# Linear attention and a gated MLP on one core: one query layout for all batches, k^T v copied once, listed buffers and another written order

## The chip, the core and the metric

The kernel runs on one core of a Trainium2 chip. Five engines work on their own instruction queues: TensorE (PE, matrix products, with its weight loads listed as PEld), VectorE (DVE), ScalarE (ACT), GpSimd (POOL) and SyncE (SP), which here only issues DMAs. The time is that of the device, in microseconds (us), from one launch; lower is better.

## The reference, cut to what matters

Eight batches (b), eight heads, 576 tokens, head dimension 64. The first half is a linear attention without softmax, the second an MLP with a gate over the tokens:

```
kv  = einsum('bhsd,bhse->bhde', k, v)          # 64 x 64 per head
out = einsum('bhsd,bhde->bhse', q, kv)
x   = out / sqrt(mean(out*out, -1) + 1e-6) * g_norm     # then (b, 576, 512)
h   = gelu_tanh(x @ w_in);  u, v = h[..., :512], h[..., 512:]
v_n = (v - mean) / sqrt(var + 1e-6) * g_ln
v_s = einsum('ts,bsd->btd', w_sg, v_n) + b_sg
y   = x + (u * v_s) @ w_out
```

## The kernel before

Everything is written out by hand. A string `ORDER` lists some 1,890 steps; a step is a letter, the batch, a number and sometimes the engine (v for DVE, a for ACT, p for POOL), and each becomes one or a few instructions at the end of its engines' queues. No scheduler moves them. An engine takes its instructions in that order and waits where an operand or a buffer is not ready.

The steps that this text speaks of, batch by batch:

- `k` and `q` load keys, values and queries; `D` loads a piece of the weights. All are issued by SP in the written order.
- `K` makes k^T v: 64 x 64 products of PE, two at a time in the two column halves, summed over the tokens in one PSUM bank (`pkv`). `c` (`kv_copy`) copies that to SBUF (`kvf`). Before, four copies per batch of 64 x 256 put each head's block where `o` wants it.
- `o` multiplies kvf with the queries (PSUM tiles `pq` in batch 0, `po` in the others); `e` squares the result on ACT, `f` scales it into `x`, `s` sums the squares over each head by products with ones (`psq`, `pss`), `t` makes the reciprocal root in small DVE steps.
- In batch 0 the roots are spread over the partitions by a product (`M`, tile `pb`) and `x` multiplies. In the other batches `r0` writes the rows to DRAM (`rd`), and further `r` read them back broadcast: `bc` for two tiles of x, and `bc` again, in the same buffer, for the other two; `bl` for the last 64 tokens.
- `X` and `Y` split x into a high part (`xh`) and the rest (`xo`), since the products run in the one-pass form of fp32 (fp32r) as three products each.
- `U` and `V` (12 matmuls each, `pu` 128x288 and `pv` 128x512) are x @ w_in; `S` (14 matmuls, `pg`) the product over the tokens; `P` (`py`, 12 matmuls) the output product with seven blocks instead of eight. `g`, `G`, `H`, `J`, `R`, `h`, `W` make the gated operand between S and P; `Q` and `Z` add py to x; `O` stores.
- `A` `B` `E` `L` `C` `F` `I` turn the words of the weights into their high and low parts on ACT, DVE and POOL, piece by piece. U needs pieces 0 to 3 of w_in, V pieces 4 to 7.
- `N` is a product of zeros into a bank that nobody reads (`warm`): it only keeps PE busy. There are 78.

Batches overlap: while batch b is in S and P, batch b+1 is in U and V, and K, o, s of b+2 lie between. PSUM has four banks `ps`, two `po`, two `pa`; a tile takes the next bank of its tag in turn. The 28 buffers `h` of 128x288 are listed by number in `HOMES`.

In batch 0 the queries come in another layout than in the others (two lines of the launch code), since there one tile of q holds one half of the tokens for two pairs of heads, so that half of the work can begin after two of the four loads.

## Time and profile before

| | |
|---|---|
| median of 3 runs | 500.01 us (499.13 to 500.21) |
| the profiled execution: its time | 499.58 us |
| its span (first to last instruction) | 497.8 us |
| PE busy | 487.7 us, 98% |
| DVE, ACT, POOL busy | 72%, 36%, 33% |

Times of rows count from the first instruction of the span. "Busy" of PE is taken from starts and modelled ends of matmuls, so it holds pipeline latency too. An fp32 product is listed as two rows (two passes), an fp32r product as one. In a row of the timeline, the bracket at the end gives the idle time of the engine before the row and who ended it.

### The profile page before, as it was taken

How to read it: one execution, taken by the hardware profiler on the slowest of the kernel's cores; microseconds unless marked ns; L12 is line 12 of the kernel's file. 1: busy time of each engine (PE TensorE's matmuls, PEld its weight loads, DVE VectorE, ACT ScalarE, POOL GpSimd, SP SyncE). 2: the span in 40 equal slices, each digit the busy share in tenths (PEclk: the TensorE clock that was granted, in tenths of full speed). 3: DMA queues.
4: the chain of work that ended last, by engine and by line, in shares of the span. 5: the costliest groups of instructions: out<-in, count | busy, mean ns of one | idle time of the engine just before them, and what ended most of it. 6: DMA issues, size and time to landing. Idle time of an engine off the chain costs nothing.

```text
span 497.8 us, 10129 instructions
## 1 busy us (share of the span) xinstructions
PE 487.7 (98%) x3998; PEld 442.6 (89%) x3998; DVE 357.6 (72%) x830; ACT 181.4 (36%) x443; POOL 164.7 (33%) x206
## 2 busy tenths in 40 slices
PE   6999999999999999999999999999999999999997
PEld 6568888999988999889998898998998799989996
DVE  2388799888886776578565788557757777557576
ACT  1478677245235312242233215124223523122121
POOL 2232235541354222522253133362153205432350
PEclk9999999999999999999999999999999999999999
DMA  8996786220543563002736325100240033000014
GB/s 232 362 324 222 208 251 183 75 90 20 176 116 114 141 181 112 1 1 78 203 118 201 101 80 180 35 1 25 60 163 0 2 84 91 0 2 0 1 49 166
DMA packets 33658, 55.36 MB, mean 111 GB/s; under 512 B 7308, under 2 KB 9228, under 8 KB 33612
## 3 DMA queue, kind: packets, MB, share of 16 engines
q1 hardware_dynamic: 33612, 54.73, 36.1%
q8 instruction: 31, 0.51, 0.4%
q14 instruction: 15, 0.12, 0.1%
HBM read 44.76 MB, written 9.95 MB: 110 GB/s over the span
## 4 chain that ended last, share of the span: by engine, by line
PE 87%; DVE 6%; DMA 3%; ACT 2%; issue 1%; SPq 0%
PE pg L639 20%; PE pu L625 19%; PE pv L574 18%; PE py L700 17%; PE pkv L365 4%; PE pg L642 3%; PE po L398 3%; PE pss L443 2%; DMA v<-in_vl 1%; DMA kv_first<-in_vx 1%; DVE g L668 1%; DMA q<-in_qT 1%; DVE xo L543 1%; PE warm L221 1%; PE psq L427 1%; PE pb L511 1%
## 5 line engine op out<-in xcount | busy, mean ns | idle before, releaser
L652 POOL TENSOR_TENSOR u<-gt,u 128x288 f32<-128x288 f32 x64 | 56.6, 893 | 98.7 <-DVE gt L647 96.2
L639 PE MATMUL pg<-wsh,vh 128*128 128x288 f32 x256 | 76.0, 297 | 0.0
L639 PE MATMUL pg<-wso,vh 128*128 128x288 f32 x256 | 75.6, 295 | 0.0
L639 PE MATMUL pg<-wsh,vo 128*128 128x288 f32 x256 | 75.5, 295 | 0.0
L713 DVE SCALAR_TENSOR_TENSOR x<-py,x 128x288 f32<-128x288 f32 x112 | 48.7, 452 | 20.3 <-PE py L700 19.7
L668 DVE TENSOR_TENSOR g<-u,g 128x288 fp32r<-128x288 f32 x112 | 53.8, 499 | 10.3 <-ACT g L176 8.1
L647 DVE SCALAR_TENSOR_TENSOR gt<-pg,glt,b_bc 128x288 f32<-128x288 f32 x64 | 32.3, 513 | 35.3 <-PE pg L642 35.2
L630 ACT ACTIVATE u<-pu 128x288 f32<-128x288 f32 x64 | 25.8, 410 | 85.3 <-PE pu L625 84.5
L700 PE MATMUL py<-g,woh 128*128 128x288 f32 x256 | 55.9, 296 | 1.0 <-DVE x L713 1.0
L176 ACT CAST g<-u 128x288 fp32r<-128x288 f32 x72 | 29.7, 433 | 62.5 <-POOL u L652 30.3
L639 PEld LDWEIGHTS pg<-wsh,vh 128*128 128x128 f32 x256 | 48.1, 188 | 0.9 <-DVE gt L647 0.4
L639 PEld LDWEIGHTS pg<-wso,vh 128*128 128x128 f32 x256 | 48.1, 188 | 0.1
L639 PEld LDWEIGHTS pg<-wsh,vo 128*128 128x128 f32 x256 | 48.2, 188 | 0.0
L625 PE MATMUL pu<-xh,wuh 128*128 128x288 f32 x256 | 45.4, 299 | 0.0
L625 PE MATMUL pu<-xo,wuh 128*128 128x288 f32 x256 | 44.5, 295 | 0.0
L625 PE MATMUL pu<-xh,wuo 128*128 128x288 f32 x256 | 44.3, 295 | 0.0
L700 PEld LDWEIGHTS py<-g,woh 128*128 128x128 f32 x256 | 42.8, 188 | 1.7 <-DVE x L713 1.4
L589 POOL TENSOR_SCALAR rs<-mv 128x1 f32<-128x1 f32 x36 | 12.7, 353 | 88.4 <-DVE mv L585 87.7
L700 PE MATMUL py<-g,wxh 128*128 128x288 f32 x192 | 41.4, 298 | 0.4 <-DVE g L668 0.4
L625 PEld LDWEIGHTS pu<-xh,wuh 128*128 128x128 f32 x256 | 37.9, 188 | 3.2 <-issue 1.0
L579 ACT ACTIVATE hv<-pv 128x512 f32<-128x512 f32 x32 | 19.0, 597 | 55.1 <-PE pv L574 51.9
L700 PE MATMUL py<-g,woo 128*128 128x288 f32 x128 | 37.8, 295 | 0.0
(124 smaller groups left out, 1043.8 us busy)
## 6 DMA issues: line engine op xcount, KB each, us to landing
q<-in_qT SPq DMA_DIRECT2D x32, 288.0 KB, 5.3
out_y<-x SPq DMA_DIRECT2D x28, 288.0 KB, 2.3
bc<-rd SPq DMA_DIRECT2D x28, 256.0 KB, 4.4
k<-in_kx SPq DMA_DIRECT2D x24, 256.0 KB, 4.0
v<-in_vx SPq DMA_DIRECT2D x24, 256.0 KB, 4.4
words<-in_wu SPq DMA_DIRECT2D x4, 512.0 KB, 3.8
kv_first<-in_kx SPq DMA_DIRECT2D x8, 256.0 KB, 6.4
kv_first<-in_vx SPq DMA_DIRECT2D x8, 256.0 KB
```

The costliest lines, as they stand in the source:

```text
L176: e.copy(dst, src) if e is ac else e.tensor_copy(dst, src)
L365: nc.tensor.matmul(part["kv", b][64 * r : 64 * r + 64, p * 64 : p * 64 + 64], k_[b, c][:, h], v_[b, c][:, h], start=(c == 0 and p == 0), s ...
L574: nc.tensor.matmul(pv, a[cc], w[:, cc, :], start=(n == 0), stop=(n == 11))
L579: ac.activation(hv_[b, c], pv_[b, c], AF.Gelu_apprx_tanh, scale=W_UP)
L625: nc.tensor.matmul(pu[:, :HS], w[:, cc, f], a[b, cc][:, t], start=(i == 0), stop=(i == 11))
L630: ac.activation(u_[b, n], part["u", b, n][:, :HS], AF.Gelu_apprx_tanh, scale=W_UP)
L639: nc.tensor.matmul(ps[:, :HS], a[:, d], w[:, c, t], start=(i == 0), stop=False)
L647: ve.scalar_tensor_tensor(g_[b, n], ps[:, :HS], glt[:, dc : dc + 1], b_bc[:, half(n // 4)], op0=ALU.mult, op1=ALU.add)
L652: po.tensor_tensor(u_[b, n], g_[b, n], u_[b, n], op=ALU.mult)
L668: ve.tensor_tensor(lo, src, f32(hi), op=ALU.subtract)
L700: nc.tensor.matmul(y_[b, bank][c][:, :HS], wo_block(h, blk, e)[:, block(c)], a, start=(start and i == 0), stop=(i == 5), skip_group_check= ...
L713: ve.scalar_tensor_tensor(xs, y_[b, bank][c][:, :HS], W_UP, xs, op0=ALU.mult, op1=ALU.add)
```

## The change

The query layout of batch 0 is taken for all batches: tile 2r + p//2 of q holds the half r of the tokens for the pairs p of heads. In `K` the head of a product is chosen so that heads land in the partition half in which `o` reads them. So k^T v leaves PSUM in one copy of 128 x 256 per batch (8 copies, not 32), kvf is half as large, and one step `o(b, n)` of a batch b > 0 makes one half of the tokens for all four pairs, from two tiles of q, where before it made both halves of two pairs. The number of products is the same. Successive products of `o` now go to the array's quarters (rows 0-63, columns 0-63), (0-63, 64-127), (64-127, 0-63), (64-127, 64-127); before, to (0-63, 0-63), (64-127, 0-63), (0-63, 64-127), (64-127, 64-127). Batch 0 had the new sequence already.

All tags with several buffers, the PSUM banks among them, now have a list in `HOMES` that says which buffer each tile takes. The buffers of tag `x` are 12, not 11. `ORDER` is written anew from end to end, with 51 steps `N`, not 78.

```diff
@@ T, PS
+    turn = {tag: iter(homes.split()) for tag, homes in HOMES.items()}
     def T(shape, dtype, tag, bufs=1, nm=None):
-        return sb.tile(shape, dtype, tag=tag, bufs=bufs, name=nm or tag)
+        home = tag + next(turn[tag]) if bufs > 1 else tag
+        return sb.tile(shape, dtype, tag=home, bufs=1, name=nm or tag)
     def PS(nm, tag="ps"):
-        return pp.tile([P, 512], F32, tag=tag, bufs=BANKS[tag], name=nm)
+        return pp.tile([P, 512], F32, tag=tag + next(turn[tag]), bufs=1, name=nm)
@@ kv
-            for p in range(NP):
+            for n in range(NP):
                 for r in range(2):
-                    h = slice(p * P + 64 * r, p * P + 64 * r + 64)
+                    h = slice((n // 2 * 2 + r) * P + n % 2 * 64, (n // 2 * 2 + r) * P + n % 2 * 64 + 64)
@@ kv_copy
-        if not n:
-            part["kvf", b] = T([P, NP, P], F32, "kvf", 2)
-        src = part["kv", b][64 * h : 64 * h + 64, : NP * 64].rearrange("a (p e) -> a p e", p=NP)
-        cast(e, part["kvf", b][64 * r : 64 * r + 64, :, 64 * h : 64 * h + 64], src)
+        part["kvf", b] = T([P, NP * 64], F32, "kvf", 2)
+        cast(e, part["kvf", b], part["kv", b][:, : NP * 64])
@@ o
-        for p in (n % 4,) if b == 0 else (2 * n, 2 * n + 1):
+        r = n // 4 if b == 0 else n
+        for p in (n % 4,) if b == 0 else range(NP):
...
+                    part["kvf", b][d, (p // 2 * 2 + h) * 64 : (p // 2 * 2 + h) * 64 + 64],
+                    q_[b, 2 * r + p // 2][d, half(h)],
@@ launch
-    qT = q.reshape(B, NP, 2, 2, HS, D).transpose(0, 1, 3, 5, 2, 4).copy()
-    qT[0] = qT[0].transpose(1, 0, 2, 3, 4).reshape(qT[0].shape).copy()
+    qT = q.reshape(B, NP, 2, 2, HS, D).transpose(0, 3, 1, 5, 2, 4)
@@ ORDER, its first line
-    D00 q00 k04 D21 D23 k00 k01 N899 N898 N897 ...
+    D00 A00 k04 B00a E00 L00 C00 k01 F00a D21 I00v F21 D23 k03 k00 N899 N898 N897 ...
```

Three places show how instructions move. The first is the head of SP's queue, the order in which the first loads are issued (`words` are weight pieces, `kv_first` keys and values of batches 0 and 1, `k<-in_kl` their last 64 tokens). Before:

```order
L238 DMA words<-in_wu 128x2x512
L385 DMA q<-in_qT 128x576
L356 DMA k<-in_kl 64x512
L356 DMA v<-in_vl 64x512
L246 DMA gnt<-in_gn 128x1
L251 DMA glt<-in_gl 128x4
L356 DMA kv_first<-in_kx 128x512
L356 DMA kv_first<-in_vx 128x512
```

and now:

```order
L289 DMA words<-in_wu 128x2x512
L407 DMA k<-in_kl 64x512
L407 DMA v<-in_vl 64x512
L407 DMA kv_first<-in_kx 128x512
L407 DMA kv_first<-in_vx 128x512
L297 DMA gnt<-in_gn 128x1
L302 DMA glt<-in_gl 128x4
L407 DMA kv_first<-in_kx 128x512
```

The first tile of q moved from second place to behind the last keys and values of batch 0 and one more piece of words.

The second is the head of PE's queue, up to the first products of U (`pb` spreads the roots of batch 0, `pkv` is batch 1's k^T v, `po` batch 1's output, `pss` its sums of squares). Before:

```order
L365 MATMUL pkv<-kv_first 64x64 x16
L365 MATMUL pkv<-v,k 64x64 x8
L511 MATMUL pb<-rstd,ext 128x288
L398 MATMUL po<-q,kvf 64x288 x8
L443 MATMUL pss<-sq,ones 32x144 x4
L398 MATMUL po<-q,kvf 64x288 x8
L625 MATMUL pu<-xh,wuh 128x288 x4
```

and now:

```order
L416 MATMUL pkv<-kv_first 64x64 x8
L416 MATMUL pkv<-v,k 64x64 x8
L554 MATMUL pb<-rstd,ext 128x288
L441 MATMUL po<-q,kvf 64x288 x8
L668 MATMUL pu<-xh,wuh 128x288 x4
L668 MATMUL pu<-xh,wuo 128x288 x4
L668 MATMUL pu<-xo,wuh 128x288 x4
L668 MATMUL pu<-xh,wuh 128x288 x4
L668 MATMUL pu<-xh,wuo 128x288 x4
L668 MATMUL pu<-xo,wuh 128x288 x4
L441 MATMUL po<-q,kvf 64x288 x8
```

The second half of batch 1's `po` and the first four products of its `pss` moved behind the first two U.

The third is DVE's queue between the roots of batch 0 and the last `xo` ahead of the first U (`x<-x,pb` scales batch 0's x, `x<-po` scales batch 1's, `w_...` and `wuo` are weight pieces). Before:

```order
L524 TENSOR_TENSOR x<-x,pb 128x288 x4
L543 TENSOR_TENSOR xo<-x,xh 128x288
L524 TENSOR_TENSOR x<-x,pb 128x288
L277 TENSOR_SCALAR w_356<-w_356 128x512
L524 TENSOR_TENSOR x<-x,pb 128x288
L281 SCALAR_TENSOR_TENSOR w_356<-words,w_356 128x512
L176 COPY kvf<-pkv 64x4x64 x2
L524 TENSOR_TENSOR x<-x,pb 128x288 x2
L420 TENSOR_SCALAR x<-po,g_66 128x288 x3
L543 TENSOR_TENSOR xo<-x,xh 128x288 x2
L334 TENSOR_TENSOR wuo<-w_333,wuh 128x2x256
L543 TENSOR_TENSOR xo<-x,xh 128x288 x2
```

and now:

```order
L567 TENSOR_TENSOR x<-x,pb 128x288 x7
L232 CAST xh<-x 128x288
L328 TENSOR_SCALAR w_326<-w_326 128x512
L586 TENSOR_TENSOR xo<-x,xh 128x288
L232 CAST xh<-x 128x288
L385 TENSOR_TENSOR wuo<-w_278,wuh 128x2x256
L586 TENSOR_TENSOR xo<-x,xh 128x288 x4
```

The two copies of kvf, three scalings of batch 1 and one step on a weight piece left this stretch; two casts came in from ACT.

Further back, the written order decides how much PE work lies between a batch's last `s` and its first U or V, that is, what PE has to do while the roots go through DRAM (counted in the order list):

| batch | before | now |
|---|---|---|
| 1 | 6 U, 5 V and three K steps | 5 U, 5 V and three K steps |
| 2 | 8 S, 3 P, K40, o30 | 8 S, 2 P, K40, o30 |
| 4 | 8 S, 6 U, 6 P, 1 V, o50, K60 | 8 S, 2 P, K61, o50 |

## Rows read from the trace of the kernel before

**Rows 1.** Busy time of PE, PEld, DVE, ACT and POOL (instructions in brackets) in three stretches, then granted clock, DMA share and GB/s: batch 0 up to its roots, from there to the first U, and the rest of the span. The first column is the stretch, the second its length.

```profile
16.80:27.30 10.50, 10.11 (x61) 4.43 (x60) 6.89 (x16) 7.99 (x19) 2.71 (x2) 1.00 1.06 355
27.30:40.04 12.74, 12.57 (x141) 7.80 (x142) 10.91 (x26) 10.08 (x23) 4.31 (x4) 1.00 1.05 326
40.04:497.80 457.76, 452.23 (x3659) 418.60 (x3656) 337.21 (x778) 161.15 (x400) 154.91 (x194) 1.00 0.31 94
```

**Rows 2.** PE's timeline behind the first U: the four places where a stream of fp32r products stood still, with the idle time and who ended it.

```profile
149.46 0.74 PE L574 MATMUL pv<-wvh,xo 128*128 128x512 f32 x2 [0.42 <-DVE xo L543]
...
179.36 0.40 PE L700 MATMUL py<-g,woh 128*128 128x288 f32 x1 [0.46 <-DVE x L713]
...
291.86 0.40 PE L700 MATMUL py<-g,woh 128*128 128x288 f32 x1 [0.51 <-DVE x L713]
...
488.08 0.53 PE L700 MATMUL py<-g,wxh 128*128 128x288 f32 x2 [0.39 <-DVE g L668]
```

**Rows 3.** PE's timeline from K of batch 0 to the first U: start, us, line, output and operands, rows of the trace in it.

```profile
14.37 1.22 PE L221 MATMUL warm<-zeros 128*128 128x256 f32 x8
...
16.12 0.68 PE L365 MATMUL pkv<-v,k 64*64 64x64 f32 x16
...
17.52 0.83 PE L398 MATMUL pq<-q,kvf 64*64 64x288 f32 x4
...
22.57 0.71 PE L398 MATMUL pq<-q,kvf 64*64 64x288 f32 x8
...
38.06 0.74 PE L443 MATMUL pss<-sq,ones 128*32 128x144 f32 x8 [0.17 <-ACT sq L410]
38.73 1.38 PE L398 MATMUL po<-q,kvf 64*64 64x288 f32 x16
40.04 0.79 PE L625 MATMUL pu<-xh,wuh 128*128 128x288 f32 x4
```

**Rows 4.** SP's timeline, its issues (start, us of the issue): the last main load of batch 0, the second and third q, and the last main load of batch 1.

```profile
8.37 0.87 SPq L356 DMA_DIRECT2D kv_first<-in_vx  x1
...
9.76 1.19 SPq L385 DMA_DIRECT2D q<-in_qT  x2
...
22.51 0.33 SPq L356 DMA_DIRECT2D kv_first<-in_vx  x1
```

**Rows 5.** The loads of keys and values in the first 30 us (all of line L356): us from the start of an issue to its landing.

```profile
DMA to landing us min/median/max: 4.4/5.6/8.2
```

**Rows 6.** DVE's timeline in the head: the last step of batch 0's roots, a step on a weight piece, the first four scalings of x, and the last two `xo` of the tiles that the first U reads.

```profile
29.14 0.45 DVE L467 SCALAR_TENSOR_TENSOR rstd<-rstd 32x288 f32<-32x288 f32 x1
29.62 0.69 DVE L281 SCALAR_TENSOR_TENSOR w<-words,w 128x512 int32<-128x512 int32 x1
...
30.95 1.75 DVE L524 TENSOR_TENSOR x<-x,pb 128x288 f32<-128x288 f32 x4
...
39.20 0.82 DVE L543 TENSOR_TENSOR xo<-x,xh 128x288 fp32r<-128x288 f32 x2
```

**Rows 7.** Groups by line and form on ACT: count, busy us, mean ns of one, idle time before them and who ended it. A step on a weight piece, the copies of kvf, the squares of batch 0.

```profile
L266 ACT ACTIVATE w<-words 128x512 f32<-128x512 f32 x8 | 5.4, 674 | 3.8 <-DMA words<-in_wu 2.3 <-DVE wvo L334 1.5
...
L176 ACT COPY kvf<-pkv 64x256 f32<-64x256 f32 x23 | 8.4, 365 | 12.6 <-PE pkv L365 12.2
...
L410 ACT ACTIVATE sq<-pq 128x288 f32<-128x288 f32 x8 | 3.1, 407 | 1.3 <-PE pq L398 0.8 <-DVE x L420 0.3
```

**Rows 8.** The same view for DVE: scalings of batch 0, and copies of kvf.

```profile
L176 DVE COPY kvf<-pkv 64x256 f32<-64x256 f32 x9 | 3.8, 418 | 9.6 <-ACT kvf L176 9.5
...
L420 DVE TENSOR_SCALAR x<-pq,g 128x288 f32<-128x288 f32 x5 | 2.4, 514 | 1.3 <-ACT sq L410 1.3
```

**Rows 9.** The way of batch 2's roots through DRAM, SP's timeline: the write of the rows and the two broadcast reads.

```profile
127.61 0.58 SPq L498 DMA_DIRECT2D rd<-rstd  x1
...
130.39 1.30 SPq L493 DMA_DIRECT2D bc<-rd  x2
...
136.90 1.24 SPq L493 DMA_DIRECT2D bc<-rd  x2
```

**Rows 10.** The same way on DVE: the scalings behind each read, and the last `xo` ahead of batch 2's first V.

```profile
135.50 1.37 DVE L527 TENSOR_TENSOR x<-x,bc 128x512 f32<-128x512 f32 x2 [0.17 <-DMA bc<-rd]
...
143.96 1.89 DVE L527 TENSOR_TENSOR x<-x,bc 128x512 f32<-128x512 f32 x2
146.76 2.64 DVE L543 TENSOR_TENSOR xo<-x,xh 128x576 fp32r<-128x576 f32 x2
```

**Rows 11.** The chain that ended last, in order of time (start, us, what): batch 2's sums, one S (12 and 2 products), one P, one V, one o with a K behind it.

```profile
122.80 1.23 PE pss L443 x32
...
126.11 1.57 PE pg L639 x12
127.69 0.26 PE pg L642 x2
127.95 1.58 PE py L700 x12
...
154.52 2.77 PE pv L574 x12
...
187.94 1.13 PE po L398 x16
189.07 1.55 PE pkv L365 x48
```

More of the change, by code (lines that the diff above doesn't have):

```diff
@@ new lines @@
+HOMES = dict(
+    pa="""
+    0 1 0 1 0 1 0 1 0 0 0 1 1 1 0 0
+""",
+    po="""
+    0 1 0 1 0 1 0 1 0 1 0 1 0 1 0 0 1 1 0 1 0 1 0 1 0 0 1 0 1
+""",
+    ps="""
[5 rows of a table added]
+""",
+    h="""
[10 rows of a table added]
+""",
+    hv="""
+    0 1 2 0 1 2 0 2 1 0 2 0 1 2 0 1 2 0 1 2 0 1 2 0 0 2 1 0 2 0 1 0 2 1 0 1 0 1 2 0
+""",
+    k="""
+    0 1 2 0 1 1 2 0 1 2 1 0 2 0 2 2 1 0 0 1 0 1 2 1 2 1 0 2 1 0 1 0
+""",
+    kvf="""
+    0 1 0 1 0 1 1 0
+""",
+    mv="""
+    0 1 2 3 0 1 3 2 0 1 3 2 0 1 2 3 1 0 3 2 1 0 3 0 1 2 3 1 0 2 3 0 1 3 2 0
@@ new lines @@
+""",
+    q="""
+    0 1 2 3 0 1 2 3 0 2 3 2 1 3 3 0 1 2 3 0 3 0 1 2 2 0 3 1 0 2 2 0
+""",
+    rs="""
+    0 1 2 3 0 1 2 3 0 1 2 3 0 1 2 3 1 0 2 3 1 0 2 1 3 0 2 1 3 0 2 3 1 0 2 3
+""",
+    st="""
+    0 1 0 1 0 1 0 1 0 1 0 1 0 1 0 1 0 1 0 1 0 1 0 1 0 1 0 1 0 1 0 1 0 1 0 1
+""",
+    v="""
+    0 1 2 0 1 1 2 0 1 2 1 0 2 0 2 2 1 0 0 1 0 1 2 1 2 1 0 2 1 0 1 0
+""",
+    vh="""
+    0 1 0 1 0 1 0 1 0 1 0 1 0 1 0 1 0 1 0 1
+""",
+    vo="""
+    0 1 0 1 0 1 0 1 0 1 0 1 0 1 0 1 0 1 0 1
+""",
+    x="""
+    0 1 2 3 6 7 4 8 5 11 9 10 9 4 10 5 9 4 10 5 1 2 0 3 7 11 6 8 4 5 10 9 0 2 1 3 6 7 8 11
@@ L197, in tile_linear_attn_gmlp @@
     part = {}
-    turn = iter(HOMES)
-    def home(nm, dtype=F32, shape=(P, HS)):
-        return T(list(shape), dtype, "h" + next(turn), nm=nm)
     def constants():
@@ L215, in warm @@
     def warm(*_):
-        tag = "po" if ("o", 1, 0) not in part else "pa" if ("kv", 2) not in part else "ps"
-        if tag == "ps" or ("warm", tag) not in part:
-            part["warm", tag] = PS("warm", tag)
+        if "warm" not in part:
+            part["warm"] = pp.tile([P, 512], F32, tag=WARM, bufs=1, name="warm")
         moving = zeros[:, :2, :].rearrange("p a b -> p (a b)")
-        nc.tensor.matmul(part["warm", tag][:, : 2 * P], zeros[:, 0, :], moving, start=True, stop=True)
+        nc.tensor.matmul(part["warm"][:, : 2 * P], zeros[:, 0, :], moving, start=True, stop=True)
     def weight(n):
@@ L264, in word_scale @@
     def word_scale(n):
-        part["w", n] = T([P, 2, 256], I32, "hv", 3, nm="w64") if n < 8 else home("w64", I32, (P, 1, 256))
+        part["w", n] = T([P, weight(n)[3], 256], I32, *(("hv", 3) if n < 8 else ("h", 28)), nm="w64")
         ac.mul(f32(part["w", n]), f32(word_pair(n)[1]), W_DOWN)
@@ L662, in split_high @@
     def split_high(b, key, src, e):
-        gs_[b, key] = [home("g", F32R) for _ in range(2)]
+        gs_[b, key] = [T([P, HS], F32R, "h", 28, nm="g") for _ in range(2)]
         cast(e, gs_[b, key][0], src)
```

202 lines of the change are left out of this document (99 added, 103 removed), and 25 rows, old and new, of tables (HOMES, h, ps).

## The prediction

> **What bounds the kernel now.** I first cut the span into stretches [rows 1]. From 40.04 us, where the first U begins, to the end PE is busy 452.23 of 457.76 us: one dense stream, in which only four places stand still, with 0.42, 0.46, 0.51 and 0.39 us of idle time [rows 2]. Behind 40.04 PE's own work is the bound, and an order that changes nothing in that work can win some 2 us there at most. DVE, at 337.21 of 457.76 us, is far from full, and ACT and POOL are further. Ahead of 40.04 it is otherwise. PE is listed as busy there too, but with work that is not bound by PE: warm products, small fp32 products, waits hidden in their modelled ends. The end of this stretch is set by a chain over the loads of batch 0, K, o, squares, sums, roots, scaling, splitting, and then the first U. DMA is full in it (share 1.05 to 1.06), DVE is busy 10.91 of the last 12.74 us and ACT 10.08. So a change can gain or lose in two ways: by the time at which the first U starts, less what PE then still has to do, and by stalls in the dense stream.
>
> **The change part by part.** The sum is made against the profiled execution, 499.58 us with a span of 497.8; the median of the runs is 0.43 us higher, so within the spread of the runs.
>
> *K of batch 0.* The last main load of batch 0 is issued at 8.37 [rows 4]; a median landing time of 5.6 us [rows 5] gives about 14.0, and K ends at 16.12 + 0.68 = 16.8 [rows 3]. Between two of its groups stand 8 warm products, 1.22 us [rows 3]. In the new order a tile of q (288 KB, 0.8 us at the 355 GB/s of rows 1) goes behind these loads, not ahead of them, and the warm products of that place are gone. With the data at about 13.5 to 14 and three groups of K of 0.6 to 0.7 us each behind them, K ends near 15.8: 1.0 earlier. That is bounded by the landing times, 4.4 to 8.2 us [rows 5], and so by some 1 us less and 2 us more.
>
> *The copy.* Four copies of 64x256 at 365 ns on ACT and 418 on DVE [rows 7, 8], two in a row on each, become one of 128x256 on DVE. No row has that shape. It has as many elements per partition as the nearest row, which gives 0.42; as many bytes as two of them, 0.84 at most. I take 0.45, since the time of a row of this kind goes with the elements in a partition: the first o can then start at about 16.4 (q, now issued behind one more piece of words, about 10.5 + 5.6, is there at 16.1). Before it was 17.52 [rows 3]. In the other batches the copies are 24 fewer, but the rows of PE's stalls name no copy [rows 2], so 9 us of ACT and DVE work are worth nothing there by themselves.
>
> *Batch 0 to its roots.* ACT sets the pace. Behind the first o it does, in the new order, squares at 0.41, steps on weight pieces at 0.67 [rows 7] and scalings at about 0.51 [rows 8]: first square at 16.9, three more with one weight step until 19.2, sums 0.6 behind, root at 20.0 to 20.5. The second four products o then stand right behind the first sums; the listed banks are free by then. Their ACT part is one weight step, four squares and three scalings, 0.67 + 4 x 0.41 + 3 x 0.51 = 3.8, and starts at 20.5 with a wait of some 0.3 for the weight piece: until 24.7. Then a root on ACT (about 0.5) and three DVE steps of 0.45 with a weight step of up to 0.69 ahead of the last: 27.2 at most, I take 26.8. Before, the last step ended at 29.14 + 0.45 = 29.6 [rows 6]. So 2.8 earlier.
>
> *From the roots to the first U.* Before: first scaling at 30.95, last `xo` that U needs at 39.20 + 0.82 = 40.02, U at 40.04 [rows 3, 6]: DVE was the chain, for 10.4 us. Now DVE's list between the same two ends holds seven scalings at 0.44, two casts at about 0.41, five `xo` at 0.41 and two steps on weight pieces, up to 0.69 each by ACT's row: 3.1 + 0.8 + 2.05 + 1.35 = 7.3, so 26.8 + 7.3 = 34.1. Two kvf copies, three scalings of batch 1 and one weight step are out of the stretch and come later, in DVE time that the dense stream leaves free.
>
> *The second way to the first U.* K of batch 1 and the first o of batch 1 now stand ahead of it on PE. The last main load of batch 1 was issued at 22.51 [rows 4] and is now one 256 KB pair later, about 23.2; landing at 28.8 (27.6 to 31.4 by rows 5); two groups of K 1.3, the copy in ACT's queue 0.9, o 1.13 and the change of form 0.25: 32.4, at worst 35.0. I take the later of the two ways plus 0.2 for waits: **U at 34.3, 5.7 earlier**, with bounds of 32.5 and 37.
>
> *What is then still to do.* Ahead of 40.04 PE did both o of batch 1; now the second one and the first quarter of `pss` stand behind. o is 40.04 - 38.73 = 1.31 [rows 3]; for `pss` 0.3 more. Together **1.6 given back**. The 27 warm products that are gone, and the other moves, lie in the stretch that is already counted. U, V, S, P, K are the same in number and shape.
>
> *Cover of the roots.* This is where the new order takes something away. Batch 2's roots go through DRAM: sums end at 124.03 [rows 11], rows written at 127.61, read at 130.39 [rows 9], scaled at 135.50 to 136.87, second read at 136.90 into the same buffer, scaled at 143.96, last `xo` at 146.76 + 2.64 = 149.40 [rows 10]: 25.4 us, and V waited for it at 149.46, the first of the four stalls. PE work between was 8 S at 1.84, 3 P at 1.58, an o and a K at 1.13 and 1.55 and 10 of V's 12 products [rows 11]. Now batch 2 has one P less, and batch 4 has 8 S, 2 P, K61 and o50, where it had 6 U, 4 P and a V more. With S 14.7, P 3.2, K and o 2.7 and 2.3 for V's first ten, the cover is about 23.0 for batch 2 and 22.6 for batch 4 (its K is a short one). How long the way must be is bounded from below by these rows: 3.6 to the write, 2.8 to the read, 5.1 to the scaling, 1.4, again 5.1 and 1.4, and 2.2 for a cast and two `xo` (an estimate: two `xo` took 2.64 beside other work): 21.6. From above by the 25.4 seen. Batch 2's way held about 2 us in which the second scaling, ready at 142, waited behind other work on DVE, so I take 23.5. Then batch 2 waits 0.5, as before, and batch 4 0.9. Batch 1 loses one U of cover (1.6); I leave it at no wait, since its second read is not issued later. **0.9 lost.** The other three stalls I leave as they are: the rows do not tell which way they go, from 1.4 gained to as much lost.
>
> The sum: 499.58 - 5.7 + 1.6 + 0.9 = **496.4**.
>
> **The rivals.**
>
> *The cover is too short (slower).* The same mechanism with the longer way. Without any wait for batch 2 and 4 the sum is 494.9, and each us of the way L beyond 23.0 and 22.6 counts once: 494.9 + 2L - 45.6. At 25.4 that is 500.1, no change; from about 25.9 on it is slower than 501, and 26.5 gives 502.3. For it: SP issues the reads in order, behind loads of k and q with waits of their own, and the 25.4 were measured. Against it: the 2 us that batch 2's way lost on DVE.
>
> *The head does not come forward.* DMA is full there [rows 1], and the same bytes must come before the first U, and of the weights of V soon after. If the loads of batch 1 land at the long end and K waits for them, U starts at 38 and the sum is 499.58 - 2.0 + 1.6 + 0.9 = 500.1. Against it: with the median landing of rows 5 K is ready 1.7 us ahead of the DVE way.
>
> [...]
>
> *The quarters of the array.* Successive products of o now share the row half. If the second of a pair had to wait for the first, o would go from four at a time to two: 14 o at 1.13 would cost up to 15.8 more, and the time would be 512.2. Against it: batch 0 already has this sequence, and two of its o, 8 rows, take 0.71 us with the last one's drain, less than the 1.13 of 16 rows would allow for pairs in turn [rows 3, 11]. [...]
>
> **How the numbers follow.** A measurement of this kernel can tell 0.2%, 1 us, from no change. Chances: the forecast 0.66, own range 494.0 to 498.8; cover too short 0.17 (half of it below 501, half above); head not forward 0.08; clock 0.06; quarters 0.03. Faster than 499.0: the forecast but for 0.02, most of the clock, and the mild ends of the cover and the head: 0.76. Slower than 501.0: 0.07 from the cover, 0.03 from the head, 0.03 from the quarters: 0.13. The rest, 0.11, within 0.2%. The range: down to 492.5 if U starts at 32.5 and the stalls shrink, up to 501.0 to take in half of the cover's case and the head's.
>
> **What the profile of the changed kernel would show.** The head: the first `pu` at 34.3 in PE's timeline (32.5 to 37), K of batch 0 done near 15.8, the last step of batch 0's roots near 26.8, one kvf copy of about 0.45. A span of about 494.6. Cover: idle PE ahead of the first V of batches 2 and 4, released by DVE `xo`, of 0.5 to 1 us; 2.5 us or more there would be the slower rival. Quarters: an o behind U of 1.1 us, not 2. Clock: 1.00 in all stretches. Wrong I would be by a wait that these rows cannot show: a listed buffer that comes free late, or a load behind a blocked SP.

## The result

The changed kernel takes 505.56 us by median (503.32 to 510.04, 4 runs), the kernel before 499.87 beside it (499.13 to 500.21, 4 runs): a ratio of 1.0126, 95% interval 1.0091 to 1.0162. (This ratio and those below are taken over all runs, so they are not quite the quotient of the two medians; the interval follows in square brackets.) It is slower; the forecast was 496.4 and faster. The profiled execution is the run of 504.42 us, with a span of 502.6.

| | before | after | forecast |
|---|---|---|---|
| K of batch 0 done | 16.80 | 18.96 | 15.8 |
| first o of batch 0 | 17.52 | 19.91 | 16.4 |
| last step of batch 0's roots done | 29.6 | 29.9 | 26.8 |
| last `xo` that the first U reads | 40.02 | 36.1 | 34.1 |
| first U | 40.04 | 38.12 | 34.3 |
| from the first U to the end | 457.76 | 464.48 | 460.3 |

So both halves missed: the first U came 1.9 us earlier, not 5.7, and the dense stream behind it grew by 6.7, not by 2.5.

**The head.** PE's timeline of the changed kernel up to the first U (start, us, line, output and operands, rows; in brackets the idle time and who ended it):

```profile
13.11 1.98 PE L416 MATMUL pkv<-kv_first 128*64 128x64 f32 x32 [5.39 <-DMA kv_first<-in_vx]
15.02 1.22 PE L272 MATMUL warm<-zeros 128*128 128x256 f32 x4
16.17 1.98 PE L416 MATMUL pkv<-kv_first 128*64 128x64 f32 x32
18.08 0.88 PE L416 MATMUL pkv<-v,k 64*64 64x64 f32 x16
...
32.09 1.92 PE L416 MATMUL pkv<-kv_first 128*64 128x64 f32 x32
...
36.98 1.20 PE L441 MATMUL po<-q,kvf 64*64 64x288 f32 x16
38.12 0.81 PE L668 MATMUL pu<-xh,wuh 128*128 128x288 f32 x4
```

K takes its groups by number, and the new order loads group 0 as the third of the four main pairs. So PE, which before began K at 8.88, stood idle for 5.39 us until 13.11, and then all five groups lay behind the landing. And two groups take 1.98 us, four warm products 1.22, where [rows 3] have eight in 1.22. The windows of the changed kernel (columns as in [rows 1]) say why:

```profile
11.90:18.40 6.50, 5.29 (x74) 4.86 (x76) 0.00 (x0) 1.24 (x2) 0.00 (x0) 0.50 1.03 386
18.60:32.20 13.60, 13.04 (x102) 6.98 (x100) 11.20 (x26) 8.48 (x20) 5.23 (x4) 1.00 1.04 298
32.30:35.60 3.30, 3.30 (x50) 2.96 (x48) 3.30 (x10) 1.88 (x5) 0.00 (x0) 0.50 1.01 353
38.12:502.60 464.48, 457.36 (x3684) 420.31 (x3680) 331.74 (x775) 155.74 (x386) 160.10 (x202) 1.00 0.31 95
```

The granted clock is 0.50 in two stretches, one that begins in the idle time and one behind a run of small fp32 products, while K of batch 0 and of batch 1 run. Before, it was 1.00 throughout. DVE was no longer the chain: its last `xo` ahead of the first U ends 2.0 us before U begins.

```profile
34.56 1.56 DVE L586 TENSOR_TENSOR xo<-x,xh 128x288 fp32r<-128x288 f32 x4
```

The loads were late too. The last main load of batch 1 is issued at 26.60, not at 23.2 as I had put it (SP's timeline), and DMA moves fewer bytes at the same busy share: a window of the changed kernel, then the same window of the kernel before; in the window from 18 to 21 it is 281 GB/s and 386. But in this execution no load holds the head after 13.11: the chain that ended last goes from K of batch 0 over its sums and roots (29.9) to the second group of `pb` products (30.44), behind which PE's queue has the rest of K of batch 1 and its o.

```profile
26.60 0.33 SPq L407 DMA_DIRECT2D kv_first<-in_vx  x1
```

```profile
21.00:24.00 3.00, 2.99 (x28) 1.26 (x24) 2.86 (x7) 2.48 (x8) 0.91 (x1) 1.00 1.07 193
```

```profile
21.00:24.00 3.00, 2.61 (x20) 0.97 (x19) 1.72 (x4) 2.30 (x7) 0.67 (x2) 1.00 1.08 311
```

**The dense stream.** Its waits of a quarter of a us or more, in PE's timeline. They answer to [rows 2], and to a fifth wait that the kernel before had ahead of a K step, which [rows 2] leaves out since its products are not fp32r (the last line here, of the kernel before):

```profile
57.61 0.68 PE L416 MATMUL pkv<-v,k 64*64 64x64 f32 x16 [0.75 <-DMA v<-in_vl]
...
77.54 0.96 PE L617 MATMUL pv<-wvh,xo 128*128 128x512 f32 x3 [1.44 <-DVE xo L586]
...
118.75 0.79 PE L668 MATMUL pu<-xh,wuh 128*128 128x288 f32 x4 [0.25 <-DVE x L756]
...
343.62 1.20 PE L617 MATMUL pv<-wvh,xh 128*128 128x512 f32 x4 [0.51 <-DVE x L756]
...
394.80 1.20 PE L617 MATMUL pv<-wvh,xh 128*128 128x512 f32 x4 [0.43 <-ACT x L461]
```

```profile
266.10 0.59 PE L365 MATMUL pkv<-v,k 64*64 64x64 f32 x13 [0.34 <-DMA v<-in_vl]
```

3.4 us of waits instead of 2.1, and the five places of before are gone. The longest is batch 1's first V; the last three, by the program, wait for a PSUM bank of the list that was still being read. That explains 1.3 of the 6.7; the second o of batch 1, now in this stretch, is 1.5 (41.50 to 42.98 in the same timeline). A third part is in no wait. Where V follows V, from the start of one V to the next it is 2.77 us now and 2.72 before (the first products of two V in a row of the changed kernel, then of the kernel before):

```profile
63.87 1.10 PE L617 MATMUL pv<-wvh,xh 128*128 128x512 f32 x4
...
66.64 1.10 PE L617 MATMUL pv<-wvh,xh 128*128 128x512 f32 x4
```

```profile
62.54 1.07 PE L574 MATMUL pv<-wvh,xh 128*128 128x512 f32 x4
...
65.26 1.07 PE L574 MATMUL pv<-wvh,xh 128*128 128x512 f32 x4
```

Over all V a product takes 0.2315 us from start to start, before 0.2284 (worked out from all starts of the trace, pauses left out): 432 products, 1.3 us. Products of U go from 0.1326 to 0.1331, 0.4 us. What is left, about 2.2, stands at no single place: by all starts of the trace, with idle time left out, S and P take some 0.4 us more each, K 0.3, the twelve other o together 0.6, V and U 0.4 beyond the rates above, and idle times under a quarter of a us are 0.3 more.

### The profile page after: what moved, and what is told of

It reads as the page before. It is cut to its first block, busy times and chain, and to the rows that moved or that the text cites. A ratio compares the mean times of both kernels' runs of the same rounds, so it can differ in the third digit from the quotient of the medians.

```text
span 502.6 us, 10052 instructions
## 1 busy us (share of the span) xinstructions
PE 487.7 (97%) x3971; PEld 442.5 (88%) x3971; DVE 350.6 (70%) x824; ACT 172.1 (34%) x420; POOL 167.5 (33%) x211
## 4 chain that ended last, share of the span: by engine, by line
PE 88%; DMA 5%; DVE 4%; ACT 2%; issue 1%; SPq 0%; DVEq 0%; ACTq 0%
PE pg L682 20%; PE pv L617 20%; PE py L743 17%; PE pu L668 17%; PE pkv L416 4%; PE pg L685 3%; PE po L441 3%; DMA v<-in_vl 2%; PE pss L486 2%; DMA kv_first<-in_vx 1%; DMA bl<-rd 1%; DVE xo L586 1%; PE psq L470 1%; PE warm L272 1%; DMA rd<-rstd 1%
## 5 line engine op out<-in xcount | busy, mean ns | idle before, releaser
L756 DVE SCALAR_TENSOR_TENSOR x<-py,x 128x288 f32<-128x288 f32 x112 | 49.1, 452 | 28.2 <-PE py L743 27.3
L690 DVE SCALAR_TENSOR_TENSOR gt<-pg,glt,b_bc 128x288 f32<-128x288 f32 x64 | 32.5, 514 | 35.6 <-PE pg L685 35.2
L232 ACT CAST g<-u 128x288 fp32r<-128x288 f32 x67 | 27.9, 433 | 77.7 <-POOL u L695 33.0
L723 POOL TENSOR_TENSOR u<-u 128x288 f32<-128x288 f32 x30 | 25.9, 867 | 48.6 <-DVE g L711 40.6
L668 PEld LDWEIGHTS pu<-xo,wuh 128*128 128x128 f32 x256 | 37.8, 188 | 0.0
```

The lines of the kernel that those rows point to most:

```text
L232: e.copy(dst, src) if e is ac else e.tensor_copy(dst, src)
L668: nc.tensor.matmul(pu[:, :HS], w[:, cc, f], a[b, cc][:, t], start=(i == 0), stop=(i == 11))
L690: ve.scalar_tensor_tensor(g_[b, n], ps[:, :HS], glt[:, dc : dc + 1], b_bc[:, half(n // 4)], op0=ALU.mult, op1=ALU.add)
L723: e.tensor_tensor(dst, x, y, op=ALU.subtract)
L756: ve.scalar_tensor_tensor(xs, y_[b, bank][c][:, :HS], W_UP, xs, op0=ALU.mult, op1=ALU.add)
```

## The experiments

Theory A, my first one: the granted clock made the head late, and the packs of warm products (several steps N in a row) that the new order dropped would have held it. Rival B: the order of the loads and of the work sets the head, and the low clock falls into waits. The edits are shown in `ORDER`, with "..." for what is unchanged.

**Warm products in the idle time.**

```diff
- ... N865 N864 K00 K01 k02 ...
+ ... N865 N864 N100 N101 N102 ... N140 N141 K00 K01 k02 ...
```

> The changed kernel with 42 more warm products ahead of the first K, in the 5.39 us in which PE stood idle (7.7 to 13.1). [...] Theory B (the order of the loads and the work sets the head, the low clock only falls into waits that are there anyway): the first U stays at 38 within 0.5, and the time is 503.5 to 506.

504.83 (501.87 to 508.20, 8 runs), ratio 1.0108 [1.0075, 1.0140]. The clock stayed at 1.00 until 30.1, and K of batch 0 ended at 16.81: 2.1 of the 3.2 us by which K missed my 15.8 were the clock. But the first U did not come forward, and the next thing that was late shows in ACT's and PE's timelines and, between them, in the chain that ended last (start, us, what):

```profile
23.87 0.66 ACT L321 ACTIVATE w<-words 128x512 f32<-128x512 f32 x1 [1.67 <-DMA words<-in_wu]
```

```profile
12.99 10.79 DMA words<-in_wu
```

```profile
25.18 1.64 PE L474 MATMUL psq<-sq,ones 128*32 128x288 f32 x6 [2.26 <-ACT sq L457]
...
39.32 0.80 PE L672 MATMUL pu<-xh,wuh 128*128 128x288 f32 x4
```

A piece of words issued at 12.99 landed at 23.8, and ACT stood at the step on it with the squares of batch 0 queued behind. Theory A is right on K and wrong on U. From 30.1 to 37 the clock was 0.50 here too.

**More packs, through the head.** More steps N at seven places, of which two:

```diff
- ... D03 s02 A03 ... B01a L01 M02 t07 ...
+ ... D03 N200 N201 N202 s02 A03 ... B01a L01 N210 ... N215 M02 t07 ...
```

> As the run with 42 more warm products ahead of the first K, and 25 more between the second sums of batch 0 and the first o of batch 1 (3 ahead of the sums, 6 and 3 around the spreading of the roots, 5, 4, 3 and 3 between the K groups of batch 1 and ahead of its o). Theory A: the granted clock is 1.00 throughout, the first U comes at 35 to 36.5, the time is 500.5 to 502.5, and the runs agree within 1 us; what then remains above 499.9 is the dense stream's (a wait of 1.6 us in batch 1's V at 77.5, one of 0.9 in K of batch 2 at 57.6). Theory B: first U at 38 or later, since the added products stand in the way, time 504 to 507.

506.03 (503.80 to 510.31, 4 runs), ratio 1.0136 [1.0073, 1.0200]. The clock is 1.00 throughout, and the first U comes at 39.00: 0.3 us earlier than with the 42 products alone (39.32), and 0.9 later than in the changed kernel (38.12). In the chain that ended last PE is continuous from 24.06 on, and 4.7 us of it are the packs. So PE itself is the chain there: at the low clock because its products run at about half speed (six rows of `pb` take 3.21 us at 0.50 with the 42 products alone, 1.72 here), at the full clock because of the packs that stand in it. The time also spreads over 6.5 us at a clock of 0.999 to 1.000, so the spread is not the clock's alone.

**The kernel before without its packs.** The 26 warm products between its groups of K left out:

```diff
- K00 N863 N862 ... N854 K01 k02 N853 ... N846 K02 ... k03 N845 ... N838 K03 K04
+ K00 K01 k02 K02 ... k03 K03 K04
```

> The kernel before without the 26 warm products between its first four groups of K. [...] Theory B: the groups of K wait for their loads as before, U stays at 40.0, and the time is 499.2 to 500.4.

502.77 (502.28 to 503.53, 4 runs), ratio 1.0058 [1.0036, 1.0081]. Nothing else was changed. A window from the second group of K on, and PE's rows of the second group of K and the first U:

```profile
14.00:24.40 10.40, 9.77 (x60) 5.35 (x60) 3.61 (x8) 3.84 (x9) 1.29 (x1) 0.51 1.06 359
```

```profile
11.74 0.69 PE L367 MATMUL pkv<-kv_first 128*64 128x64 f32 x16 [2.12 <-DMA kv_first<-in_vx]
...
43.09 0.80 PE L627 MATMUL pu<-xh,wuh 128*128 128x288 f32 x4
```

PE idles 2.12 and then 0.85 and 0.66 us between groups, the clock is 0.51 from 14.0 to 24.4, and the first U is 3.1 later. This part of theory A is shown: the packs are worth about 3 us where they stand in idle time.

**The layout without the order.** The kernel before and its `ORDER`, with the changed kernel's `kv`, `kv_copy`, `o` and query layout, and 12 buffers of x; the steps renamed to the tiles that o now makes.

> The kernel before with its own order, and only the layout changed: one query layout, one copy of k^T v per batch, o by halves of the tokens, 12 buffers of x; the squares, scalings and the four sums of batch 1 are renamed to the tiles that o now makes, three scalings stand a little earlier. If the layout itself is harmless (both theories A and B put the loss on the order): 498.5 to 501, with 24 copies less on ACT and DVE that nobody waited for, and an o of 16 rows at 1.13 to 1.3 as before. If the layout costs (products of o that take the array's quarters in turn, theory C): 14 o at up to 1.1 more each, 503 to 515.

505.41 (502.42 to 508.03, 4 runs), ratio 1.0108 [1.0048, 1.0168]. A window, and the rows of its one new long wait on PE and DVE:

```profile
272.90:279.70 6.80, 6.19 (x52) 4.45 (x52) 2.81 (x5) 2.56 (x7) 3.28 (x4) 0.50 0.29 82
```

```profile
273.51 1.33 PE L392 MATMUL po<-q,kvf 64*64 64x288 f32 x8 [1.97 <-DVE x L414]
```

```profile
272.94 0.52 DVE L414 TENSOR_SCALAR x<-po,g 128x288 f32<-128x288 f32 x1 [6.11 <-DMA out_y<-x]
```

The layout is not free under the old order. One step o now begins all four tiles of x, so the buffers of x are wanted earlier, and a scaling waited for a store of an older tile. PE stood for 1.97 us, in which the clock fell to 0.50 for 6.8 us, and from the first U to the end it is 462.6 where the kernel before has 457.8. By all starts, idle time left out, only o, `pss` and U take longer there (0.8, 1.1 and 1.6 us), which are what runs at the low clock; S and V take what they took before. The head ran at the low clock from 30.5 to 44.1 too in this execution. So neither 498.5 to 501 nor theory C came true: an o of 16 rows is no longer than before (36.98 to 38.12 in the changed kernel, 1.14). What the layout is worth by itself stays open, since no run of it was free of low clock.

**The loads of the last rows.** Theory D came from the windows of GB/s above: the loads `ext`, k and v of batch 1's last 64 tokens, all to 64 partitions, were issued from 14.32 to 16.41, in a row. With the 42 warm products, and:

```diff
- ... D22 ... k14 s04 ... k13 N851 ...
+ ... D22 ... s04 ... k13 k14 N851 ...
```

> The changed kernel with the 42 warm products ahead of the first K, and the loads of the last 64 keys and values of batch 1 issued behind the four main pairs of batch 1 (as the kernel before has it), not ahead of them. Theory D (the loads): these two and ext, all to 64 partitions and issued one behind the other, hold up the DMA engines (281 and 193 GB/s from 18 to 24 where the kernel before has 386 and 311), so that the piece of words issued at 12.99 landed at 23.8 and held ACT ahead of the squares. Then the piece now lands by 21.5, PE's wait for the second squares shrinks from 2.3 to under 1, the second roots are done by 28 (29.5 with the 42 products alone), and the first U comes at 36 to 38. Rival (only the sum of the bytes matters): the piece still lands at 23 to 24 and the first U stays at 39 to 39.5. The time follows U: 501.5 to 503.5, or 504 to 506.

502.98 (501.88 to 508.33, 10 runs), ratio 1.0066 [1.0030, 1.0101]. The window of above and the first U:

```profile
21.00:24.00 3.00, 2.42 (x22) 0.79 (x20) 2.90 (x8) 2.48 (x7) 0.00 (x0) 1.00 1.06 322
```

```profile
35.03 0.80 PE L672 MATMUL pu<-xh,wuh 128*128 128x288 f32 x4
```

322 GB/s where the warm products alone had 185 (312 for 289 in the window ahead of it), the roots of batch 0 done at 28.2 and not at 29.5, no wait for words, PE's wait for the squares 0.6, and the first U at 35.03, even earlier than theory D's 36 to 38. Not all of that is the loads': of the 4.3 us against the run with the 42 products alone, 1.3 are there when the roots are done, and the other 3.0 come behind them, where that run had the clock at 0.50 from 30.1 to 37 and this one has 1.00. That the loads keep the clock up is not shown, since only five of the ten runs average 0.999 or more; the profiled one is among them and is the fastest. With the loads and the clock in order the head comes forward by 5.0 us, near what I had forecast. And the profiled run still takes 501.88: from the first U to the end it is 465.1.

That the 64 partitions of these loads make it is not shown: no run here took such a load by itself.

**The same loads moved early in the kernel before.**

```diff
- ... D22 A01 k10 ... x04v X04a k14 C01 ...
+ ... D22 k14 A01 k10 ... x04v X04a C01 ...
```

> The kernel before with the loads of the last 64 keys and values of batch 1 issued right behind ext, ahead of three main pairs of batch 1. Theory D: GB/s between 18 and 24 falls from 386 and 311 toward 280 and 200, the last main load is issued and lands some 2 us later, and the first U comes 0.5 to 2 us later (40.5 to 42): 500 to 502. Rival: the order of these loads does not matter, 499.2 to 500.2, U at 40.0.

500.97 (498.67 to 504.72, 10 runs), ratio 1.0007 [0.9974, 1.0041]. Two windows, and SP's issue of the last main load (22.51 in [rows 4]):

```profile
21.00:24.00 3.00, 2.61 (x19) 0.98 (x21) 1.72 (x4) 2.32 (x7) 0.66 (x2) 1.00 1.08 237
24.00:27.00 3.00, 3.00 (x17) 1.30 (x15) 2.05 (x5) 2.60 (x7) 0.80 (x1) 1.00 1.08 180
```

```profile
27.66 0.33 SPq L359 DMA_DIRECT2D kv_first<-in_vx  x1
```

GB/s falls right behind these loads, to 237 and 180 where the kernel before moved 311 and 350, and the last main load is issued 5.1 us later. In the kernel before a dip comes too, later, behind the same two loads at 24.56 and 25.17: 236 GB/s from 27 to 30. So the effect on DMA is shown; that on the time is not (the interval holds 1), and the first U of the profiled run, 43.93, had the low clock in it, so it tells nothing about the loads.

**Two edits behind the first U.** Theory E: DVE and POOL slow each other.

```diff
- ... F16a K21 I07v E08 D18 F18a V01 ... Y12v Y13p Y11v V10 ...
+ ... F16a I07v E08 D18 F18a V01 K21 ... Y12v Y13v Y11v V10 ...
```

> The changed kernel with two edits behind the first U: the xo of tile 3 of batch 1 on DVE, not POOL, and the second K step of batch 2 one V later. Theory E (DVE and POOL slow each other): while POOL made its xo (2.06 us) two DVE xo took 1.99 and 1.28 us where 0.75 is the rule; with all four on DVE at 0.75 the last ends near 76.4 and PE's wait in batch 1's first V falls from 1.44 to 0.3 or less. Rival (the way of the roots through DRAM is late, whoever makes xo): the wait is 1.2 to 1.7. The K step: its wait of 0.7 for v goes (1.0 saved in all), or the wait moves to another step. From the first U to the end 462 to 463 us (464.5 now) if both work, and 502 to 503.5 by median where the changed kernel had 505.6; the runs still differ by some us, since the head is left as it is.

506.25 (501.86 to 509.28, 10 runs), ratio 1.0097 [1.0061, 1.0133]; the head is the changed kernel's, and the granted clock averages 0.976 to 0.997 in the ten runs. From the first U to the end the profiled run takes 464.5, not the 462 to 463 expected, but 3.2 us of that are at the clock of 0.50. The two waits tell more: the K step K21 no longer waits, and V waits 0.6, not 1.44; in the kernel with all edits (below), 0.89. That is half of what theory E promised. First the `xo` of the changed kernel on DVE and POOL's work beside them, then the same with all `xo` on DVE (the kernel with all edits, below):

```profile
73.62 3.86 DVE L586 TENSOR_TENSOR xo<-x,xh 128x576 fp32r<-128x576 f32 x3
```

```profile
73.60 2.06 POOL L586 TENSOR_TENSOR xo<-x,xh 128x576 fp32r<-128x576 f32 x1 [5.55 <-ACT xh L232]
75.62 1.24 POOL L335 TENSOR_TENSOR w<-w,words 128x256 int32<-128x256 int32 x1
```

```profile
71.41 3.31 DVE L591 TENSOR_TENSOR xo<-x,xh 128x576 fp32r<-128x576 f32 x4
```

```profile
71.56 1.20 POOL L340 TENSOR_TENSOR w<-w,words 128x256 int32<-128x256 int32 x1 [4.87 <-DVE w L337]
```

The three DVE rows are 0.75, 1.99 and 1.28 us long, and they alternate with POOL's: the first ends at 74.37, POOL's at 75.66, the second DVE row 0.62 later, POOL's next at 76.86, the third again 0.62 later. One waits while the other works. With all four on DVE a sum of words on POOL still makes one of them 1.31.

**The same `xo` on POOL in the kernel before** (`Y13v` becomes `Y13p`, nothing else).

> The kernel before with one edit: the xo of tile 3 of batch 1 on POOL, as the new order has it. Theory E (DVE and POOL slow each other): POOL's xo takes about 2.0 us, and a DVE xo that runs beside it 1.3 to 2.0 where it took 0.75; V of batch 1 has enough cover here, so the time stays at 499.2 to 500.5. Rival: the DVE rows stay at 0.75 and the long ones in the changed kernel had another reason.

500.58 us in its one run. POOL, then DVE:

```profile
71.69 2.11 POOL L543 TENSOR_TENSOR xo<-x,xh 128x576 fp32r<-128x576 f32 x1 [4.22 <-PE pv L574]
```

```profile
71.77 0.75 DVE L543 TENSOR_TENSOR xo<-x,xh 128x576 fp32r<-128x576 f32 x1
72.68 1.66 DVE L612 TENSOR_TENSOR vo<-hv,vh 128x512 fp32r<-128x512 f32 x1 [0.16 <-ACT vh L176]
```

POOL's 2.11 came as expected. The one `xo` beside it took 0.75, as the rival has it, but the next DVE row, `vo`, took 1.66 where the `vo` behind it takes 0.68; it ended 0.55 behind POOL's row. So DVE's 0.75 went first, POOL's own part is the 1.3 behind it, and then came `vo`. What POOL takes with no DVE row beside it shows further back in the changed kernel, 1.4 us a tile:

```profile
430.30 4.19 POOL L586 TENSOR_TENSOR xo<-x,xh 128x576 fp32r<-128x576 f32 x3
```

So "they slow each other" was the wrong picture and "they take turns, whole instructions at a time" fits all three.

**All edits together.** The 42 warm products, the late loads, `xo` on DVE, K21 one V later, and 6 warm products ahead of s02 and 4 ahead of M07.

```diff
- ... D03 s02 ... k14 s04 ... L01 M07 ... k13 N851 ... K21 I07v ... V01 D19 ... Y12v Y13p ...
+ ... D03 N200 ... N205 s02 ... s04 ... L01 N210 ... N213 M07 ... k13 k14 N851 ... I07v ... V01 K21 D19 ... Y12v Y13v ...
```

> Both of the edits above behind the first U, the late loads of the last rows, the 42 warm products, and ten more at two places where PE waits anyway (6 ahead of the second sums of batch 0, 4 ahead of the product that spreads the second roots). If the clock, the loads and the two waits are what made the changed kernel slower: granted clock 1.00, first U at 35 to 37, from there 462 to 463, time 498.5 to 501, equal to the kernel before or a little faster. If the head is bound by the sum of the bytes: U at 38.5 to 39.5, time 501.5 to 503.5.

501.35 (499.45 to 503.31, 12 runs) against 500.19, ratio 1.0013 [0.9985, 1.0041]: with four repairs the changed kernel is level with the kernel before. The clock is 0.999 or 1.000 in all twelve runs. The first U comes at 36.39, 1.4 later than in the kernel with late loads and without the ten packs, and from there it is 463.1, so 5.4 longer than before.

**One U more to hide the roots of batch 1.** Theory F. The second o of batch 1 goes ahead of the second U:

```diff
- ... U00 u00 L04 e16 C04 B06a q13 o11 e13 A08 U03 D10 e11 s10 ... s13 t10
+ ... L04 e16 C04 B06a q13 o11 e13 A08 U00 D10 e11 s10 ... s13 U03 t10
```

> The changed kernel with all edits so far (42 warm products, late loads of the last rows, xo on DVE, the K step one V later), six packs of one warm product, not ten, at the two places in the head, and the second o of batch 1 ahead of the second U, its first sums ahead of the third: so the roots of batch 1 start one U earlier and its V has one U more to hide them. Theory F (batch 1's cover is what the new order shortened): PE's wait of 0.9 in batch 1's first V goes to 0.2 or less, first U at 35 to 36.5, from there 461.5 to 462.5, time 498.5 to 500.5. Rival (the way of the roots is held by its second read, whose place in SP's queue sets it): the wait stays at 0.6 to 1.0 and o makes PE wait for the squares ahead of it; time 500 to 502.

503.28 (502.07 to 505.49, 12 runs), ratio 1.0057 [1.0035, 1.0080]. The run doesn't decide on theory F: this kernel, other than the expectation says, still had the `xo` of tile 3 on POOL, its lists of banks and of buffers `h` had to change with the order, and o in its new place stood twice, for a load of q and for a bank:

```profile
39.08 0.72 PE L446 MATMUL po<-q,kvf 64*64 64x288 f32 x8 [0.85 <-DMA q<-in_qT]
40.50 0.72 PE L446 MATMUL po<-q,kvf 64*64 64x288 f32 x8 [0.70 <-ACT x L466]
```

Behind these waits the clock was 0.50 from 41.5 to 45.0. Half of the sums were done 8.6 us behind the first U, not 7.2, and V waited 1.4 as in the changed kernel.

**The roots' steps closed up.** Theory G. The steps t11 to t18 of batch 1, among which the new order puts steps on `xo`, weights and casts, now follow each other but for one pair X, Y; r10 goes ahead of a pair of loads.

```diff
- t10 ... U01 t11 X01a Y01v I20v t12 t13 n01 ... K20 t14 t15 f17a t16 t17 E10 t18 ... f15a r10
+ t10 ... U01 t11 t12 t13 X01a Y01v t14 t15 t16 t17 t18 I20v n01 ... u01 r10 D12 k23 ...
```

> The kernel with ten more warm products and all edits (501.35 by median; xo on DVE), and the nine DVE steps of batch 1's roots closed up: between the first sums and the write of the rows the new order puts steps on xo, on weight pieces and casts among them, so that the write is issued 7.1 to 8.1 us behind the first sums, where it is 4.4 in the kernel before; the write also goes ahead of a pair of loads. Theory G (the way of batch 1's roots is late because its steps are spread, not because the cover is a U shorter): the write comes 5.0 to 6.5 us behind the first sums, all that follows moves forward with it, and PE's wait of 0.9 in batch 1's first V falls to 0.2 or less; from the first U to the end 462.2 or less (463.1 before). Rival: the second read or its landing stays where it is and the wait is 0.6 to 1.0. The time: 500 to 501.

500.91 (499.88 to 502.57, 12 runs), ratio 1.0022 [1.0005, 1.0038]. SP's issue of the write of the rows (first in the changed kernel, then here), and what PE waits for here:

```profile
52.44 0.65 SPq L541 DMA_DIRECT2D rd<-rstd  x1
```

```profile
47.85 0.65 SPq L546 DMA_DIRECT2D rd<-rstd  x1
```

```profile
71.63 0.69 PE L421 MATMUL pkv<-v,k 128*64 128x64 f32 x16 [0.96 <-DMA v<-in_vx]
...
265.17 0.73 PE L622 MATMUL pv<-wvh,xh 128*128 128x512 f32 x2 [1.33 <-ACT xh L237]
```

The write comes 4.6 us behind the middle of the sums (14.3 - 7.2 = 7.1 in the changed kernel, 8.04 - 3.60 = 4.4 before, counted from the first U), 3.6 us earlier than in the kernel with all edits, and V of batch 1 no longer waits. But what lies behind the write did not move forward with it. SP's issue of the second read, first here, then in the kernel with all edits:

```profile
64.18 1.24 SPq L541 DMA_DIRECT2D bc<-rd  x2
```

```profile
63.12 1.24 SPq L541 DMA_DIRECT2D bc<-rd  x2
```

Counted from the first U the second read comes 1.3 us later, and the last `xo` is done only 0.3 earlier (38.0, not 38.3). The rest of V's 0.89 is hidden by a K step right ahead of it that waits 0.96 for its load. That wait is not the edit's: the first run of the next experiment, whose order is that of all edits, has it too, at 1.06, and there V waits 0.92 as well:

```profile
71.87 0.69 PE L423 MATMUL pkv<-v,k 128*64 128x64 f32 x16 [1.06 <-DMA v<-in_vx]
```

So theory G is not shown: the steps closed up, the reads stayed where they were, as its rival has it. And batch 4's first V waits 1.33. In the changed kernel batch 4 did not wait, in the two kernels with other places in SBUF (below) 0.2 and 0.5: this cover is just enough or just not.

**The places in SBUF.** First an unused tile of 64 words ahead of all others, which moves nearly all buffers by 256 bytes; then the eight tiles of xh and xo allocated first, side by side.

```diff
+    for tag in ("xh", "xo"):
+        for i in range(NP):
+            sb.tile([P, S], F32R, tag=tag + str(i), bufs=1, name=tag)
     gnt = T([P, 1], F32, "gnt")
```

> The kernel with ten more warm products and all edits (501.35 by median), and an unused tile of 64 words per partition allocated ahead of all others, so that nearly every buffer in SBUF stands 256 bytes further on; the order is the same but for one memset. Question: in all kernels with the new order a product of V takes 0.2315 to 0.2320 us from start to start, in those with the old order 0.2284. If the place of the operands in SBUF makes it: the mean changes by 0.001 or more, one way or the other, and the time by some 0.5 us. If something else does (the stream of instructions, waits): 0.2315 to 0.2320 again, and the time within the spread of the runs.

501.18 (499.71 to 502.72, 10 runs), ratio 1.0013 [0.9987, 1.0039]; a product of V takes 0.2315 us. No difference.

> The kernel with ten more warm products and all edits (501.35 by median), with nothing changed but the place of the four xh and four xo tiles in SBUF: they lie side by side, xh from 1,152 to 10,368 bytes, where the new order scatters xh (76,992, 82,752, 98,112 and 107,968; the kernel before has them at 67,776 to 76,992); other buffers move with them. In the new order the products of V with xh take up to 0.240 us, those with xo 0.227. If the scattered places make it: the mean of V's products goes from 0.2318 to 0.2285 and some 1 to 2 us come back, 499.5 to 500.5. If not: 0.2310 to 0.2320, and 500.5 to 502.

501.10 (499.24 to 502.32, 10 runs), ratio 1.0014 [0.9993, 1.0035]. Two V that follow each other here:

```profile
61.35 1.08 PE L625 MATMUL pv<-wvh,xh 128*128 128x512 f32 x4
...
64.09 1.08 PE L625 MATMUL pv<-wvh,xh 128*128 128x512 f32 x4
```

2.74 us, between 2.77 and 2.72; over all V 0.2298 a product, 0.2317 in the same kernel with scattered tiles (0.2315 to 0.2321 in every other run with the new order), and U's 0.1325 as before the change. So where the buffers lie costs something: by these rates some 0.8 us on V and 0.4 on U came back; with the longer steps between V's products counted too it is 0.4 on V. That xh alone makes it is not shown, since other buffers moved with it, and not quite half of V's excess is left. By median the time is no other than without this edit, since waits of 0.9, 0.7 and 0.5 remain.

## Why the prediction was wrong

*K of batch 0 (failed).* I wrote "With the data at about 13.5 to 14 and three groups of K of 0.6 to 0.7 us each behind them, K ends near 15.8". Five groups lay behind the landing of group 0 at 13.1, since it is loaded third; at the full clock that ends at 16.8 (the run with 42 warm products). The other 2.1 us are the clock. The diff showed both, the order of the k steps and the packs gone from between them; I took the packs for work that was saved.

*The copy (right).* 0.42 us on DVE and 0.37 on ACT where I took 0.45: as long as the copies of half the partitions, 0.418 and 0.365 [rows 7, 8]. *Batch 0 to its roots (right in size):* 10.0 us from the first o to the last step, 10.4 forecast, all of it shifted by K. *From the roots to the first U (right for DVE, and not the end):* 6.2 us where I had 7.3. *The second way to the first U (failed):* I had it at 32.4, "at worst 35.0", and it ended at 38.12. I took the two ways as independent and the later one as the end. In PE's queue they stand one behind the other: most of K of batch 1 comes behind the second group of `pb` products, which needs the roots, and they were done 3.1 us later than forecast. From there K ran at the clock of 0.50 until 35.6. The last main load was issued 3.4 us later than I put it, behind three slow loads, but K did not wait for it here. The forecast of 34.3 is almost reached in the run with the loads moved and a clock of 1.00: 35.03.

*The rivals.* The clock, at 0.06 among the chances, was a main part of the mechanism in the head: at 0.50 it hit K of both batches, which stands in the chain. "The head does not come forward" put U at 38, and 38.12 came, by luck: its way, K of batch 1 waiting for its loads, is not in the chain. "The quarters" did not happen: an o of 16 rows takes 1.14. The slower rival, cover too short, was right in kind and wrong in place. (Without any wait of batches 2 and 4 its sum is 495.0 by its own terms, not 494.9; nothing hangs on that.)

*What is then still to do (right).* 1.6 given back, of which o alone is 1.5.

*Cover of the roots (failed in place).* Batches 2 and 4, priced at 0.5 and 0.9, do not wait. Batch 1 I left "at no wait, since its second read is not issued later": counted from the first U that read comes 26.4 us behind, before 20.4. Its sums come 3.6 later and the nine DVE steps take 2.7 longer among other work; but the read came no earlier when these steps were closed up, so what holds it stays open. The wait that followed is 1.44; 0.5 to 0.8 of it went when all `xo` were made on DVE, so that part is POOL's turn.

*The other stalls and the rate of PE (no term).* I left the dense stream as it was, and [rows 2], from which I took "only four places stand still", had missed a fifth of 0.34. Three waits for listed banks, one for a load, and a slower V and U are together some 3.6 us, set against five old waits of 2.1 that are gone. The bank that comes free late I had named as what would prove me wrong, but not priced.

By sums: U +3.8 late against the forecast, batch 1 +1.4 and batches 2 and 4 -0.9, V's and U's rate +1.7, waits for banks and a load, less the five old ones, -0.2, and 2.2 spread over S, P, K, o, V and U: 8.0, and 504.42 - 496.4 is 8.0.

**What stays open:** why runs of the same kernel spread by 5 us and more even at a clock of 1.00, what the layout is worth alone, the rest of V's excess, what sets the second read of batch 1's roots, and why the 2.2 us are spread over the products. No version here beats the kernel before.

## What to carry to other kernels

Idle time of PE in a head that waits for loads need not be free: 5.39 us of it were followed here by a clock of 0.50 and a K that ended 2.1 us later than at 1.00. Price what comes next at that clock, and don't book packs of warm products as savings before you have put something else in their place (26 of them left out: the first U 3.1 us later); but a pack that stands in PE's chain costs its own length, 4.7 us of the chain in the run with packs through the head. When loads are reordered, count what each one holds up, and not by its bytes alone: two small ones moved back took a window from 185 GB/s to 322. Two ways that end at the same product are not independent when they share an engine's queue. And when an order is written anew, take each batch's way of the roots from its sums to its last operand step by step, the reads' places in SP's queue among them: closing up the first part alone moved the last operand by 0.3 us.
